# Two decode layers on one core: the order of MLP loads, of scores and transposes, and the filling of the weight ring

## The chip, the cores and the metric

The kernel runs on one core of one Trainium2 chip. The metric is the device time of one execution in microseconds, the median over runs. Five engines work side by side, each through its own queue in order: TensorE (PE, with its weight loads shown as PEld), VectorE (DVE), ScalarE (ACT), GpSimd (POOL) and SyncE (SP). SP does nothing here but issue DMAs; sixteen DMA engines carry each of them.

## What is computed

Two layers, each an attention over a cache and then a gated MLP, both with a layer norm in front and a residual sum behind. There are 4 sequences with one new token each, width 640, 32 heads of 128, a window of the last 1024 cached positions, and an MLP of 1728 hidden units. Everything is float32. Both layers use the same weights and the same cache.

```python
def _A_ref(x, k_cache, v_cache, wq, wo):
    q = (x @ wq).reshape(B, Sq, Hq, Dh).transpose(0, 2, 1, 3)
    k, v = k_cache[:, :, Sk - W:, :], v_cache[:, :, Sk - W:, :]     # W = 1024
    scores = jnp.einsum("bhqd,bhkd->bhqk", q, k) * (Dh ** -0.5)
    o = jnp.einsum("bhqk,bhkd->bhqd", softmax(scores), v)
    return o.transpose(0, 2, 1, 3).reshape(B, Sq, Hq * Dh) @ wo
def _B_ref(x, W_gate, W_up, W_down):
    gate, up = x @ W_gate, x @ W_up
    return (gate * (gate > 0) * up) @ W_down
x = x + _A_ref(_layernorm(x), ...)
x = x + _B_ref(_layernorm(x), ...)      # and both once more
```

## The kernel before, in words

The host lays the weights out so that each load is a plain block of 128 partitions. A head is 9472 columns of float32 per partition: 640 of Wq, 4096 of K, 4096 of V, 640 of Wo. The MLP's 1728 hidden units are cut into three blocks of 512 units (5120 columns of W_gate and W_up, then 2560 of W_down) and the 192 units that are left over. Of these the gate and up columns (1920) and the first 128 rows of W_down (640 columns) lie in the array `rest`, and the last 64 rows of W_down lie in the array `tail`, which is 64 partitions by 640.

In on-chip memory there is one tile, `store`, of 128 partitions by STORE columns (5.76 heads), used as a ring. The list `todo`, made by `pieces`, `half_a`, `half_b`, `ending` and `mlp`, says in which order the pieces are loaded; `load()` (line 129) takes the next piece, places it at `at`, and issues its DMA on SP (line 152) if those columns are free. `done()` frees columns once the matmul that reads them has been written, and calls `load()` again. A piece that would not fit before the end of the ring is cut at one of the places in `CUTS`; a piece whose columns are not all free waits whole. On the chip the DMA waits on SP for the PE instruction that read those columns last, and, since eight semaphores go round, for the eighth DMA before it. SP is in order, so what waits there holds up every later load.

Five heads (27 to 31) are kept on chip from layer 0 to layer 1 (of head 27 only Wq and K), in columns 0 to 42,624; layer 1 takes them first. So the MLP of layer 0 and the first heads of layer 1 have only the upper 12,000 columns to pass through, until layer 1 has used up the kept heads.

The order of work on the engines is the order of the program text (`manual_schedule`). `attention` (line 322) goes through the heads; one round for head h, with `after` = h + 1 and `before` = h − 1, is: `query` of after (`qp`, line 248), `turned` of h (eight transposes of the softmax weights `probs` into `pp`, line 284, copied to `pT`, line 285), `totals` and `values_turned` of before (`so`, lines 301 and 309), `query_turned` of after (`qt`), `project` of before (`y`, line 318), `scores` of after (`ps`, line 269, then the maximum `nm` on DVE, line 274, and the exponential into `probs` on ACT, line 276), and `values` of h (`po`, line 294, copied to `gates` on ACT, line 297). There is one `probs`, one `ps`, one `po` and one `gates`.

`forward` (line 354) is the MLP: `gate(j)` multiplies by W_gate and W_up of block j (`gu`, line 365; j = 3 is the left-over units), `gated` makes the hidden values, `hidden` transposes them (`ph`, `hT`), and `down` multiplies by W_down into the sum `y` (line 404). The norm in front of each is `normalized` (line 199) with `deviation`.

Of the kernel before, what the change touches and what calls it, by code (L numbers as in the profile page):

```python
# [7 lines left out]
F32 = mybir.dt.float32  # L8
# [19 lines left out]

STORE = 54600
# [5 lines left out]
FIRST, FIRST_MLP = 10960, 51152  # L37
# [5 lines left out]
    "rest": [*range(0, RGU, P), RGU, RGU + D],  # L43
    "tail": [0, D],
# [4 lines left out]
def decode_kernel(ctx: ExitStack, tc: tile.TileContext, x, heads, blocks, rest, tail, sel, out):  # L49
# [34 lines left out]
    def mlp(layer):  # L84
        fine = layer == 0
# [42 lines left out]
    source = {"head": heads, "block": blocks, "rest": rest, "tail": tail}  # L128
# [3 lines left out]
    def load():  # L132

        nonlocal at
        while todo:
# [6 lines left out]
            if any(live[at:at + hi - lo]):  # L142
                return
# [6 lines left out]
            p = 64 if kind == "tail" else P  # L150
            src = src[i][:, lo:hi] if kind in ("head", "block") else src[:, lo:hi]
            nc.sync.dma_start(out=store[:p, at:at + hi - lo], in_=src)
# [87 lines left out]
    qp, qs, qT, pT, sums, so, r, oT = {}, {}, {}, {}, {}, {}, {}, {}  # L240
# [21 lines left out]
    def scores(layer, h):  # L262
# [3 lines left out]
        for j in range(2):  # L266
            for b in range(B):
# [3 lines left out]
                done(key, lo, 512)  # L271
        nm = small.tile([P, 1], F32, name="nm")
        flat = ps.rearrange("p j n -> p (j n)")
# [48 lines left out]
    def attention(layer):  # L322
        hs = order[layer]
        xT, d = normalized()
# [5 lines left out]
        scores(layer, hs[0])  # L330
        for h, after, before in zip(hs, hs[1:], [None] + hs):
# [22 lines left out]
    def forward(layer):  # L354
        xT, d = normalized()
# [22 lines left out]
        def hidden(j, h):  # L378
            hTs[j] = small.tile([P, 4, B], F32, name="hT")
# [6 lines left out]
            for g in range(3):  # L386
                lo = 64 * (g % 2)
                nc.tensor.matmul(ph[lo:lo + 64, g // 2, :B], h, ident[:96, 32 * g:32 * g + B],
                                 start=True, stop=True, tile_position=(0, lo))
            nc.vector.tensor_copy(hTs[j][:, 0], ph[:, 0, :B])  # L390
            nc.vector.tensor_copy(hTs[j][:64, 1], ph[:64, 1, :B])

        def down(j, groups, last=False):
            for f in groups:
                p = P
                if j < 3:
                    key, lo = (layer, "block", j), GU + f * D
                elif f == 0:
                    key, lo = (layer, "rest", 0), RGU
                else:  # L400
                    key, lo, p = (layer, "tail", 0), 0, 64
                w = get(key, lo, D)
                for g in range(4):
                    nc.tensor.matmul(y[32 * g:32 * g + B], hTs[j][:p, f], w[:p, g * QUARTER:(g + 1) * QUARTER],  # L404
                                     start=False, stop=last and f == groups[-1], tile_position=(0, 32 * g))
                done(key, lo, D)

# [3 lines left out]
        h3 = gated(3)  # L411
        gate(0)
        hidden(3, h3)
        h0 = gated(0)
        down(3, [1, 0])
        gate(1)
        hidden(0, h0)
# [78 lines left out]
```

## Time and profile before

| what | before |
|---|---|
| median of 3 runs (757.96 to 759.31) | 757.97 us |
| the profiled execution's own time | 759.14 us |
| its span | 757.3 us |
| TensorE busy, mean granted clock | 576.2 us (76%), 0.838 |
| VectorE, ScalarE busy | 175.1 us (23%), 120.5 us (16%) |
| loads on the SP queue | 315.19 MB, 98.3% of 16 engines' span |

The page counts what the engines and the DMA engines did between the first and the last instruction. A row of a timeline has the start in us, the duration, the engine, the line, the operation and its tiles; in brackets stands how long the engine had been idle and what ended the wait. Matmuls of float32 appear as two instructions each. A row of the windows has the busy time of each engine, the granted TensorE clock, the mean busy share of the 16 DMA engines, and the GB/s that they moved.

### The profile page before, as it was taken

What the parts mean: (1) busy time and instruction counts of PE and PEld (TensorE: products, weight loads), DVE (VectorE), ACT (ScalarE), POOL (GpSimd) and SP (SyncE); (2) the same over time, 40 slices, a digit from 0 to 9 for tenths busy, and PEclk for the clock granted to TensorE, in tenths of its full rate; (3) what the DMA queues carried; (4) which work ended last, traced back from release to release, by engine and by line L of the source; (5) the groups of instructions that cost most, each with busy time, mean ns of one, the idle gap of its engine ahead of it and who ended that gap; (6) DMA issues with size and microseconds to landing.
All of it is one profiled execution on the core that took longest, in us unless ns stands there. A gap on an engine that the chain in (4) does not pass through costs nothing.

```text
span 757.3 us, 11694 instructions
## 1 busy us (share of the span) xinstructions
PE 576.2 (76%) x5146; PEld 317.1 (42%) x5146; DVE 175.1 (23%) x497; ACT 120.5 (16%) x214; POOL 0.2 (0%) x4
## 2 busy tenths in 40 slices
PE   0776777776797695798877888888778776795985
PEld 0343344344354253354433444444335344354442
DVE  0222222222222222223202223232222222221220
ACT  1111101011101101112201111211110111111120
POOL 0000000000000000000000000000000000000000
PEclk9888898788877979879976889999797788877898
DMA  9999999999999999999999999999999999999995
GB/s 389 438 416 440 428 433 429 429 432 428 435 427 428 432 435 426 425 428 421 362 395 422 365 415 426 428 440 426 425 433 433 431 429 432 429 428 424 420 398 211
DMA packets 18938, 316.02 MB, mean 417 GB/s; under 512 B 2116, under 2 KB 2756, under 8 KB 5832
## 3 DMA queue, kind: packets, MB, share of 16 engines
q1 hardware_dynamic: 18736, 315.19, 98.3%
q8 instruction: 40, 0.66, 0.4%
q10 hardware_dynamic: 152, 0.10, 0.0%
q14 instruction: 10, 0.08, 0.0%
HBM read 315.19 MB, written 0.08 MB: 416 GB/s over the span
## 4 chain that ended last, share of the span: by engine, by line
DMA 66%; PE 24%; DVE 5%; issue 3%; ACT 2%; ACTq 0%; DVEq 0%; SPq 0%
DMA store<-in_heads 58%; PE ps L269 7%; DMA store<-in_blocks 6%; PE pp L284 5%; PE so L309 4%; DVE nm L274 3%; DMA sel_sb<-in_sel 2%; PE y L318 2%; ACT probs L276 1%; PE qp L248 1%; PE qt L258 1%; DVE pT L285 1%; PE gu L365 1%; PE po L294 1%; PE y L404 1%
## 5 line engine op out<-in xcount | busy, mean ns | idle before, releaser
L269 PE MATMUL ps<-store,qT 128*32 128x512 f32 x1024 | 166.7, 783 | 1.0 <-DVE qT L260 1.0
L276 ACT ACTIVATE probs<-ps,nm 128x1024 f32<-128x1024 f32 x64 | 71.3, 1113 | 543.0 <-DVE nm L274 543.0
L294 PE MATMUL po<-store,pT 128*32 128x512 f32 x1024 | 123.6, 602 | 0.0
L274 DVE TENSOR_REDUCE nm<-ps 128x1 f32<-128x1024 f32 x64 | 78.4, 1225 | 184.9 <-PE ps L269 184.9
L248 PE MATMUL qp<-store,xT 128*32 128x128 f32 x640 | 45.1, 309 | 90.9 <-DMA store<-in_heads 89.6
L284 PE MATMUL pp<-sel_sb,probs 128*128 128x128 f32 x512 | 86.2, 323 | 23.3 <-ACT probs L276 23.2
L309 PE MATMUL so<-sel_sb,gates 128*128 128x1 f32 x512 | 80.4, 278 | 28.5 <-DVE r L303 25.2
L309 PEld LDWEIGHTS so<-sel_sb,gates 128*128 128x128 f32 x512 | 76.7, 230 | 32.9 <-issue 28.7
L248 PEld LDWEIGHTS qp<-store,xT 128*32 128x32 f32 x640 | 29.0, 118 | 139.3 <-issue 125.3
L284 PEld LDWEIGHTS pp<-sel_sb,probs 128*128 128x128 f32 x512 | 67.9, 164 | 40.9 <-ACT probs L276 33.5
L294 PEld LDWEIGHTS po<-store,pT 128*32 128x32 f32 x1024 | 34.2, 117 | 91.5 <-issue 90.8
L269 PEld LDWEIGHTS ps<-store,qT 128*32 128x32 f32 x1024 | 36.8, 135 | 71.6 <-issue 60.3
L254 DVE TENSOR_SCALAR qs<-qp,rstd 128x128 f32<-128x128 f32 x64 | 22.5, 351 | 152.4 <-PE qp L248 152.1
L285 DVE COPY pT<-pp 128x128 f32<-128x128 f32 x128 | 37.3, 292 | 65.5 <-PE pp L284 59.3
L297 ACT COPY gates<-po 128x512 f32<-128x512 f32 x64 | 36.9, 576 | 8.3 <-PE po L294 8.3
L318 PE MATMUL y<-store,oT 128*4 128x160 f32 x512 | 35.8, 360 | 1.6 <-DVE oT L312 0.5
L312 DVE TENSOR_TENSOR oT<-so,r 128x4 f32<-128x4 f32 x64 | 10.4, 162 | 98.1 <-PE so L309 98.1
L365 PE MATMUL gu<-store,xT 128*32 128x256 f32 (+1 forms) x300 | 22.6, 445 | 9.7 <-DMA store<-in_blocks 8.8
L258 PE MATMUL qt<-sel_sb,qs 128*128 128x4 f32 x128 | 28.3, 291 | 1.0 <-DVE qs L254 1.0
L258 PEld LDWEIGHTS qt<-sel_sb,qs 128*128 128x128 f32 x128 | 25.6, 248 | 1.6 <-ACT rstd L232 0.9
L301 PEld LDWEIGHTS so<-sel_sb,sm 128*128 128x128 f32 x128 | 24.0, 233 | 1.7 <-issue 1.7
L301 PE MATMUL so<-sel_sb,sm 128*128 128x4 f32 x128 | 21.1, 235 | 0.0
(49 smaller groups left out, 111.9 us busy)
## 6 DMA issues: line engine op xcount, KB each, us to landing
store<-in_heads SPq DMA_DIRECT2D x37, 4736.0 KB, 39.9
store<-in_heads SPq DMA_DIRECT2D x15, 2368.0 KB, 38.9
store<-in_heads SPq DMA_DIRECT2D x12, 1344.0 KB, 11.1
store<-in_heads SPq DMA_DIRECT2D x12, 1024.0 KB, 10.7
store<-in_blocks SPq DMA_DIRECT2D x3, 2560.0 KB, 26.9
store<-in_heads SPq DMA_DIRECT2D x2, 3648.0 KB, 38.9
store<-in_heads SPq DMA_DIRECT2D x2, 3392.0 KB, 37.8
store<-in_heads SPq DMA_DIRECT2D x1, 4656.0 KB, 39.6
```

The costliest lines, as they stand in the source:

```text
L248: nc.tensor.matmul(qp[h][32 * g:32 * g + 32, :], xT[:, c], w, start=c < 4, stop=c > 0, tile_position=(0, 32 * g))
L258: nc.tensor.matmul(qt, qs.pop(h), sel_b, start=True, stop=True)
L269: nc.tensor.matmul(ps[32 * b:32 * b + 32, j, :], q[:, b:b + 1].to_broadcast([P, 32]), get(key, lo, 512), start=True, stop=True, tile_posit ...
L274: nc.vector.tensor_reduce(nm, flat, axis=AX.X, op=ALU.max, negate=True)
L276: nc.scalar.activation(probs, flat, AF.Exp, bias=nm, accum_out=sums[h])
L284: nc.tensor.transpose(pp[:, c, :], probs[:, (4 * j + c) * P:(4 * j + c + 1) * P], ident)
L285: nc.vector.tensor_copy(t[:, 4 * j:4 * j + 4], pp[:, :, None, 0:P:32].to_broadcast([P, 4, 8, B]))
L294: nc.tensor.matmul(po[32 * g:32 * g + 32, :], p[:, c], get(key, VV + c * 512, 512), start=c < 4, stop=c >= 4, tile_position=(0, 32 * g))
L297: nc.scalar.copy(gates, po)
L301: nc.tensor.matmul(so[h][:, :B], sums.pop(h).to_broadcast([P, P]), sel_s, start=True, stop=True)
L309: nc.tensor.matmul(s[:, B + b:B + b + 1], gates[:, b * P:(b + 1) * P], sel_b[:, b:b + 1], start=True, stop=True)
L318: nc.tensor.matmul(y[32 * g:32 * g + B], o, get(key, WO + g * QUARTER, QUARTER), start=False, stop=last, tile_position=(0, 32 * g))
```

## The change

There are four edits. The `tail` array goes: its 64 rows of W_down are folded to 128 partitions by 320 columns and appended to `rest`, so that the left-over units are one load of 2880 columns (`REST`); `hidden(3)` writes its 64 left-over values to both halves of the partitions, and `down(3)` takes the upper and the lower half in four matmuls of 64 rows. In the MLP, in both layers, all of W_gate and W_up is loaded ahead of all of W_down, each in two pieces of 2048 and 3072 columns, and `down(0)` comes after `gate(2)` in the program. In a round of attention `scores` of head h + 1 comes ahead of `totals` and `turned` of head h, and the softmax is a function of its own behind these. And `load(True)` is called at the start of `attention` and `forward`: there a piece whose columns are only partly free is cut at the last place in `CUTS` that fits, if that is 512 columns or more. STORE is 40 columns smaller, FIRST and FIRST_MLP are other offsets.

```diff
+REST = RGU + D + 2 * QUARTER
-STORE = 54600
+STORE = 54560
-FIRST, FIRST_MLP = 10960, 51152
+FIRST, FIRST_MLP = 10928, 51688
...
-        gu = [0, GU * 2 // KC, GU] if fine else [0, GU]
-        pieces(layer, "rest", 0, 0, RGU)
+        gu = [0, GU * 2 // KC, GU]
+        pieces(layer, "rest", 0, 0, REST)
         pieces(layer, "block", 0, *gu)
-        pieces(layer, "tail", 0, 0, D)
-        pieces(layer, "rest", 0, RGU, RGU + D)
         pieces(layer, "block", 1, *gu)
+        pieces(layer, "block", 2, *gu)
         pieces(layer, "block", 0, GU, GU + WD)
-        pieces(layer, "block", 2, *gu)
         pieces(layer, "block", 1, GU, GU + WD)
         pieces(layer, "block", 2, GU, GU + 2 * D, GU + 3 * D, GU + WD)
...
-    def load():
+    def load(part=False):
...
             if any(live[at:at + hi - lo]):
-                return
+                n = live.index(True, at) - at
+                hi = max([lo] + [c for c in CUTS[kind] if c <= lo + n])
+                if not part or hi < lo + 512:
+                    return
...
             query(layer, after, xT)
             query_out(after, rstd)
-            turned(h)
             if before is not None:
-                totals(before)
                 values_turned(before)
             query_turned(after)
             if before is not None:
                 project(layer, before, False)
             scores(layer, after)
+            totals(h)
+            turned(h)
+            softmax(after)
             values(layer, h)
 
         before, h = hs[-2:]
-        totals(before)
+        totals(h)
+        turned(h)
         values_turned(before)
-        turned(h)
-        totals(h)
         values(layer, h)
...
+            if j == 3:
+                w = get(key, RGU + D, 2 * QUARTER)
+                for g in range(4):
+                    r = slice(64 * (g // 2), 64 * (g // 2) + 64)
+                    nc.tensor.matmul(y[32 * g:32 * g + B], hTs[j][r, 1], w[r, g % 2 * QUARTER:(g % 2 + 1) * QUARTER],
+                                     start=False, stop=False, tile_position=(r.start, 32 * g))
+                done(key, RGU + D, 2 * QUARTER)
...
+        h = gated(3)
+        for j, j1 in (3, 0), (0, 1), (1, 2):
+            gate(j1)
+            hidden(j, h)
+            h = gated(j1)
+            if j == 3:
+                down(3)
+        down(0)
+        hidden(2, h)
+        down(1)
+        down(2, last=True)
```

In the order that the built programs have, the rows of one engine stand one below the other; "x8" is eight equal instructions in a row. One round of attention on PE before (`qp`, `pp`, `so` for the totals, `so` for the values, `qt`, `y`, `ps`, `po` as above):

```order
L248 MATMUL qp<-store,xT 32x128 x5
L284 MATMUL pp<-sel_sb,probs 128x128 x8
L301 MATMUL so<-sel_sb,sm 128x4
L309 MATMUL so<-sel_sb,gates 128x1 x4
L258 MATMUL qt<-sel_sb,qs 128x4
L318 MATMUL y<-store,oT 4x160 x4
L269 MATMUL ps<-store,qT 32x512 x8
L294 MATMUL po<-store,pT 32x512 x8
```

The same round on PE in the changed kernel, whose line numbers are three higher from the softmax on:

```order
L248 MATMUL qp<-store,xT 32x128 x5
L312 MATMUL so<-sel_sb,gates 128x1 x4
L258 MATMUL qt<-sel_sb,qs 128x4
L321 MATMUL y<-store,oT 4x160 x4
L269 MATMUL ps<-store,qT 32x512 x8
L304 MATMUL so<-sel_sb,sm 128x4
L287 MATMUL pp<-sel_sb,probs 128x128 x8
L297 MATMUL po<-store,pT 32x512 x8
```

The totals and the transposes have moved from behind the query to behind the scores. On DVE the copies `pT` thereby stand directly ahead of the maximum `nm` (they stood behind `qs`, ahead of `oT`):

```order
L306 RECIPROCAL r<-so 128x4
L288 COPY pT<-pp 128x128 x2
L277 TENSOR_REDUCE nm<-ps 128x1
L254 TENSOR_SCALAR qs<-qp,rstd 128x128
L315 TENSOR_TENSOR oT<-so,r 128x4
L260 COPY qT<-qt 128x4
```

So the maximum over the new scores now waits for both copies of the head before.

The SP queue through the MLP of layer 0 before, from the load of the left-over units to the last of W_down (PE_49 is a wait for a PE instruction, DMAHW one for an earlier load):

```order
L152 DMA store_82<-in_rest 128x1920 [waits DMAHW6_49,PE_49]
L152 DMA store_82<-in_blocks 128x1280 [waits DMAHW7_49,PE_49]
L152 DMA store_82<-in_blocks 128x768 [waits DMAHW0_49]
L152 DMA store_82<-in_blocks 128x3072 [waits DMAHW1_49]
L152 DMA store_82<-in_tail 64x640 [waits DMAHW2_49]
L152 DMA store_82<-in_rest 128x640 [waits DMAHW3_49]
L152 DMA store_82<-in_blocks 128x2048 [waits DMAHW4_49]
L152 DMA store_82<-in_blocks 128x3072 [waits DMAHW6_49,DMAHW5_49,PE_49]
L152 DMA store_82<-in_blocks 128x1280 [waits DMAHW7_49,PE_49]
L152 DMA store_82<-in_blocks 128x1280 [waits DMAHW1_49,DMAHW0_49,PE_49]
L152 DMA store_82<-in_blocks 128x2048 [waits PE_49]
```

The same queue in the changed kernel:

```order
L152 DMA store_82<-in_rest 128x2560 [waits DMAHW7_49,PE_49]
L152 DMA store_82<-in_rest 128x320 [waits DMAHW0_49]
L152 DMA store_82<-in_blocks 128x2048 [waits DMAHW1_49]
L152 DMA store_82<-in_blocks 128x3072 [waits DMAHW2_49]
L152 DMA store_82<-in_blocks 128x2048 [waits DMAHW3_49]
L152 DMA store_82<-in_blocks 128x1536 [waits DMAHW4_49]
L152 DMA store_82<-in_blocks 128x1536 [waits DMAHW7_49,DMAHW5_49,PE_49]
L152 DMA store_82<-in_blocks 128x1280 [waits DMAHW6_49,PE_49]
L152 DMA store_82<-in_blocks 128x768 [waits DMAHW1_49,DMAHW0_49,PE_49]
L152 DMA store_82<-in_blocks 128x3072 [waits DMAHW2_49]
```

The `tail` load is gone, and the second 3072 columns of block 1 are cut in two at the norm, so that 1536 of them go out ahead of the first wait for the MLP's own matmuls. The load of 1280 columns behind that goes to ring columns 53,184 to 54,464, which hold the first W_down rows of the left-over units: the PE instruction that it waits for is `down(3)`, where the 1280 columns of before waited for `gate(0)`.

The end of the program on PE, in layer 1's MLP, before:

```order
L365 MATMUL gu<-store,xT 32x256 x20
L382 MATMUL ph<-sel_sb,gates 128x128
L404 MATMUL y<-store,hT 4x160 x16
L382 MATMUL ph<-sel_sb,gates 128x128
L404 MATMUL y<-store,hT 4x160 x16
```

and in the changed kernel:

```order
L371 MATMUL gu<-store,xT 32x256 x20
L388 MATMUL ph<-sel_sb,gates 128x128
L402 MATMUL y<-store,hT 4x160 x16
L388 MATMUL ph<-sel_sb,gates 128x128
L402 MATMUL y<-store,hT 4x160 x32
```

Between `gate(2)` and the end stood 32 matmuls of W_down (blocks 1 and 2); now there are 48 (all three blocks), and the loads of all three now come behind those of `gate(2)`.

More of the change, by code (lines that the diff above doesn't have):

```diff
@@ L42, with decode_kernel @@
     "block": [*range(0, GU, 256), *range(GU, GU + WD + 1, D)],
-    "rest": [*range(0, RGU, P), RGU, RGU + D],
-    "tail": [0, D],
+    "rest": [*range(0, RGU, P), RGU, RGU + D, REST],
 }
 @with_exitstack
-def decode_kernel(ctx: ExitStack, tc: tile.TileContext, x, heads, blocks, rest, tail, sel, out):
+def decode_kernel(ctx: ExitStack, tc: tile.TileContext, x, heads, blocks, rest, sel, out):
     nc = tc.nc
@@ L127, in decode_kernel @@
     at = FIRST
-    source = {"head": heads, "block": blocks, "rest": rest, "tail": tail}
+    source = {"head": heads, "block": blocks, "rest": rest}
     held = {}
-    def load():
+    def load(part=False):
         nonlocal at
@@ L149, in load @@
             src = source[kind]
-            p = 64 if kind == "tail" else P
-            src = src[i][:, lo:hi] if kind in ("head", "block") else src[:, lo:hi]
-            nc.sync.dma_start(out=store[:p, at:at + hi - lo], in_=src)
+            src = src[:, lo:hi] if kind == "rest" else src[i][:, lo:hi]
+            nc.sync.dma_start(out=store[:, at:at + hi - lo], in_=src)
             at += hi - lo
@@ L323, in attention @@
         hs = order[layer]
+        load(True)
         xT, d = normalized()
@@ L354, in forward @@
     def forward(layer):
+        load(True)
         xT, d = normalized()
```

51 lines of the change are left out of this document (15 added, 36 removed).

## Prediction

> **What bounds the kernel now.** I read the page first, then share and rate of the DMA engines by windows, then the chain of waits, and last the timeline of one round of attention.
>
> ```profile
> span 757.3 us, 11694 instructions
> q1 hardware_dynamic: 18736, 315.19, 98.3%
> DMA 66%; PE 24%; DVE 5%; issue 3%; ACT 2%; ACTq 0%; DVEq 0%; SPq 0%
> store<-in_heads SPq DMA_DIRECT2D x37, 4736.0 KB, 39.9
> 460.00:700.00 240.00, 190.57 (x1607) 104.89 (x1606) 59.15 (x160) 38.64 (x69) 0.00 (x0) 0.83 1.00 429
> 376.00:381.00 5.00, 4.48 (x78) 3.04 (x74) 1.30 (x7) 1.38 (x3) 0.00 (x0) 0.75 0.70 239
> 381.00:417.00 36.00, 24.45 (x308) 12.17 (x300) 5.73 (x22) 4.14 (x8) 0.00 (x0) 0.74 1.01 419
> 417.00:432.00 15.00, 13.23 (x122) 6.48 (x122) 4.72 (x12) 3.36 (x6) 0.00 (x0) 0.92 0.91 347
> 722.00:734.00 12.00, 9.18 (x126) 6.21 (x119) 2.71 (x13) 3.85 (x7) 0.00 (x0) 1.00 1.00 371
> 734.00:742.00 8.00, 7.42 (x137) 4.02 (x136) 1.45 (x7) 1.30 (x4) 0.00 (x0) 1.00 1.02 430
> ```
>
> The loads fill 98.3% of the DMA engines' span and two thirds of the chain: the kernel streams weights. The last two columns of a window are DMA share and GB/s. From 460 to 700 the share is 1.00 at 429 GB/s: nothing is to be had there. A head is issued 39.9 us before it lands, and its 4.85 MB take 11.3 us at 429 GB/s, so three heads wait in the queue and columns freed 3 us earlier or later are not noticed. Four places remain. The stream runs thin in the MLP of layer 0 (376 to 381, share 0.70) and early in layer 1 (417 to 432, 0.91); in the MLP of layer 1 it is busy but slow (722 to 734, 371 GB/s at share 1.00); and there is work behind the last load.
>
> ```profile
> 717.36 28.73 DMA store<-in_blocks
> 746.22 4.47 PE gu L365 x40
> 751.22 1.27 PE y L404 x32
> 729.21 0.33 SPq L152 DMA_DIRECT2D store<-in_blocks  x1
> store<-in_blocks SPq DMA_DIRECT2D x1, 320.0 KB, 23.1
> 753.02 1.31 PE y L404 x32
> 754.35 0.33 DVE probs L434
> ```
>
> The last load was issued at 729.21 and landed 23.1 us later, at 752.3. But PE takes up the last block of W_down only at 753.02: `gate(2)` could start at 746.22, when its weights had landed (717.36 + 28.73 = 746.09), and two blocks of W_down come after it.
>
> **The tail of layer 1.** Now 7680 columns of W_down (3.93 MB, 9.2 us at 429 GB/s) land behind the weights of `gate(2)`, whose 4.47 us are over well before them; each block of W_down costs PE 1.3 us, and its load 3.1. Behind the last landing there remain four matmuls, a quarter of 1.31 us, and some 0.1 us of wait: y ends 0.45 us after the landing instead of 2.0 (752.3 to 754.33). That is 1.5 us at full clock, and about 0.3 less if those matmuls run at half clock. I take 1.3. The copy and the store behind y stay.
>
> **The half load.** From 722 to 734, with the 64-partition `tail` load on its way, the stream loses 12 × (1 − 371/429) = 1.6 us; from 734 on, with 2560-column loads still coming, it runs at 430 again. The fold gives the same bytes to all partitions in longer rows, so it can lose nothing; the gain lies between 0 (another cause in that window) and 1.6. I take 1.4, near the upper end, because short rows alone did not slow the window after it. In layer 0 the same gain buys nothing by itself, for there the stream waits for PE.
>
> [...]
>
> **One round of attention.** Where PE is the slower side, the round decides when columns come free. At full clock, before:
>
> ```profile
> 424.42 1.02 PE so L309 x8
> 425.97 1.90 PE L269 MATMUL ps<-store,qT 128*32 128x512 f32 x16
> 428.00 1.22 DVE L274 TENSOR_REDUCE nm<-ps 128x1 f32<-128x1024 f32 x1 [2.14 <-PE ps L269]
> 429.32 1.11 ACT L276 ACTIVATE probs<-ps,nm 128x1024 f32<-128x1024 f32 x1 [6.14 <-DVE nm L274]
> 430.43 0.58 ACT L297 COPY gates<-po 128x512 f32<-128x512 f32 x1
> 430.58 1.09 PE L284 MATMUL pp<-sel_sb,probs 128*128 128x128 f32 x8 [0.58 <-ACT probs L276]
> 431.28 0.73 DVE L285 COPY pT<-pp 128x128 f32<-128x128 f32 x2 [0.88 <-PE pp L284]
> 431.51 0.28 PE L301 MATMUL so<-sel_sb,sm 128*128 128x4 f32 x2
> 432.24 1.05 PE L309 MATMUL so<-sel_sb,gates 128*128 128x1 f32 x8 [0.45 <-DVE r L303]
> ```
>
> From `ps` to `so` of the values 6.27 us, from there to the next `ps` 1.55 (424.42 to 425.97): 7.82, with PE idle for 0.58 + 0.45. After: `ps` about 1.7, totals 0.28, transposes until both copies are done 1.43 (430.58 to 432.01), together 3.4. Only then comes the maximum, 1.22; the exponential 0.10 later, 1.11; on ACT behind it the copy of `gates`, 0.58; `so` about 0.06 later, at 6.5; plus 1.55 makes 8.05. Both waits of PE are gone, and one of about 1.1 us for `gates`, with `so`, `qt` and `y` queued behind it, stands in their place: a round is 0.2 us longer, not shorter. What is won is a start, since `scores` no longer stand behind transposes that wait for a softmax.
>
> ```profile
> 322.49 1.91 PE pp L284 x8
> 324.98 1.84 PE so L309 x8
> 374.70 0.50 PE y L318 x8
> 383.50 0.84 PE L404 MATMUL y<-store,hT 64*4 64x160 f32 x16 [0.32 <-DVE hT L391]
> 389.14 12.66 DMA store<-in_blocks
> 414.55 1.98 PE pp L284 x8
> 416.99 3.17 PE ps L269 x16
> 427.07 0.33 SPq L152 DMA_DIRECT2D store<-in_heads  x1
> 427.00:428.00 1.00, 1.00 (x14) 0.26 (x8) 0.00 (x0) 0.00 (x0) 0.00 (x0) 1.00 0.24 81
> 428.00:429.00 1.00, 1.00 (x16) 0.28 (x12) 0.99 (x1) 0.00 (x0) 0.00 (x0) 1.00 1.03 226
> 719.00 1.90 PE L269 MATMUL ps<-store,qT 128*32 128x512 f32 x16
> 730.11 0.46 PE L318 MATMUL y<-store,oT 128*4 128x160 f32 x8 [0.26 <-DVE oT L312]
> ```
>
> **From layer 0 to layer 1** these shifts add up on one chain, and where it ends is where the stream starts anew.
> The end of attention, 375.2 before: `scores` of head 27 2.5 us earlier (322.49 to 324.98); the round behind it, partly at half clock, 1.3 longer (with 2.9 for `ps` and 2.3 for transposes and copies, as at 416.99 and 414.55, the sum above gives 10.3 instead of 9.0); three more rounds, 0.2 each; the end, 719.00 to 730.57 or 11.6 in layer 1, about 1.0 longer, since the last softmax now waits for the transposes of the head before. Together +0.4.
> The MLP of layer 0: 1536 columns more go out before PE begins (0.79 MB, 1.8 us), but the 1280 columns two places on now wait for `down(3)`, the first half of the row at 383.50, so until 383.9 + 0.4 = 384.3. All later loads of SP are queued behind; between, the stream has one load of 1536 columns. A restart costs 1.0 us from issue, and 0.5 more at the reduced rate (427.07, then 81 and 226 GB/s): in effect 385.8. From there 12,800 columns (6.55 MB) at 419 GB/s end at 401.4, with landing and the engines' spread about 402.4; before, the last landing was 389.14 + 12.66 = 401.8. So layer 1 starts 0.6 later (0 to 2).
> Early in layer 1: `scores` of head 28 no longer wait for the transposes, 2.4 earlier (414.55 to 416.99), the round behind it 1.3 longer. The load that waits at 427.07 for head 29's K is then issued at 427.07 + 0.6 − 1.1 = 426.6. By that time the stream is at 385.8 + 34,432 columns (17.6 MB) at 419 GB/s = 427.9, so it does not run dry a second time: full rate from about 428.0 where it was 428.5 before. The gain is 0.5 us. Its bounds: the whole loss of the two windows, 5 × (1 − 239/429) + 15 × (1 − 347/429) = 5.1 us won; and 2.5 us lost, if start and wait go wrong by 2 and the rounds by 0.2 each.
>
> **What is hidden or nothing.** The filling at the norms cuts a load in attention and MLP of layer 0 and none in layer 1, by the order; in the first it only splits a load that stands far ahead in the queue. The number of loads is the same. The extra matmul of `hidden(3)` and the copy that is saved (0.1 us each) lie in the wait above. In all other rounds the 39.9 us of queue cover the 0.2.
>
> **The sum.** 0.5 + 1.4 + 1.3 = 3.2 us. The profiled execution took 759.14, 1.8 more than its span and 1.2 more than the median: 759.1 becomes 755.9, and the median 757.97 becomes 754.8. Less than 0.2% (1.5 us) can't be told from no change here.
>
> **Rivals.**
> *The vector engine's order makes the rounds slow (slower).* The maximum behind two copies and `gates` behind the exponential leave PE idle 1.1 us at a stretch; if its clock is then at half more often, `ps`, transposes and `so` double on that path. By the restart some six rounds have passed; it becomes slower than now by 0.2% where each takes 0.8 us more than I reckon. At 1.0 more the transition costs 5.5, the time is 760.8. Against it: PE was idle for as much in a round before, at clock 0.92.
> *The wait for `down(3)` counts in full.* If head 29 comes no earlier, both stalls stand: about 2 us lost in place of 0.5 won, 757.3.
> [...]
> *Both thin windows fill.* If PE runs the left-over units at full clock, `down(3)` comes 1.5 us earlier and half of the 5.1 us is won: 752.8.
>
> **How the numbers follow.** Forecast 0.43, slow rounds 0.18, the wait in full 0.15, own bytes only 0.14, both filled 0.10. Nearly all of the first and last, and three quarters of the fourth, are faster: 0.64; the wait in full is mostly the same: 0.17; slow rounds give 0.19 with the rest. The likeliest alone spans 753.3 to 756.4. The range reaches down to the filled windows and up over the wait in full into the slow rounds: 752.3 to 759.5.
>
> **What the profile will show.** `y` ends about 0.5 us after the last landing; the MLP of layer 1 runs at over 420 GB/s throughout; rounds near 8 us with PE waiting for `gates` ahead of `so`; one gap in the loads between 381 and 386, none near 420. I am wrong if the gap is longer than 5 us, if rounds reach 9 us at full clock, or if the rate in layer 1's MLP stays at 400.

## The result, and the profile after

The changed kernel takes 759.13 us (median of 12 runs, 754.85 to 761.78); the kernel before, beside it, 757.97 (12 runs). The ratio, which is not the quotient of the two medians, is 1.0005 with a 95% interval of 0.9981 to 1.0029: no difference that can be told, and at most 1.4 us won where 3.2 were forecast. Six of the 12 runs took 754.9 to 757.8 us and six 760.4 to 761.8, so the median lies between two groups and no run took it. The profile is of one that took 760.87, and so shows what the slower half loses.

The page of the changed kernel, and its windows (busy time of PE, PEld, DVE, ACT and POOL, granted clock, DMA share, GB/s):

```profile
span 758.8 us, 11659 instructions
q1 hardware_dynamic: 18864, 315.19, 98.0%
DMA 54%; PE 31%; DVE 5%; ACT 5%; issue 4%; SPq 0%; ACTq 0%; DVEq 0%
376.00:381.00 5.00, 4.44 (x62) 3.52 (x61) 1.28 (x7) 1.42 (x3) 0.00 (x0) 0.50 0.70 256
381.00:384.00 3.00, 3.00 (x42) 1.34 (x34) 0.06 (x1) 0.00 (x0) 0.00 (x0) 0.69 0.62 240
384.00:386.00 2.00, 1.73 (x40) 0.92 (x40) 0.45 (x2) 0.37 (x1) 0.00 (x0) 1.00 0.03 8
386.00:388.00 2.00, 2.00 (x37) 0.93 (x27) 0.00 (x0) 0.12 (x1) 0.00 (x0) 1.00 0.89 223
417.00:432.00 15.00, 12.94 (x100) 6.35 (x104) 3.04 (x9) 2.63 (x5) 0.00 (x0) 0.77 0.93 364
460.00:700.00 240.00, 198.13 (x1632) 99.04 (x1624) 60.04 (x162) 40.36 (x72) 0.00 (x0) 0.84 1.00 429
722.00:734.00 12.00, 11.01 (x94) 5.22 (x95) 3.15 (x10) 1.68 (x3) 0.00 (x0) 0.88 1.01 420
734.00:742.00 8.00, 6.56 (x87) 4.69 (x83) 1.77 (x9) 2.73 (x5) 0.00 (x0) 0.71 1.01 424
```

The loads' part of the chain has fallen from 66% to 54%, and TensorE's has grown from 24% to 31%. From 722 to 734 the stream now runs at 420 GB/s, where it ran at 371. But in the MLP of layer 0 there are two microseconds with next to no transfer (384 to 386, 8 GB/s), and two more at about half the rate.

The chain of waits, at both ends of a layer (start, duration, what the time went to):

```profile
377.46 1.92 PE gu L371 x25
380.68 3.37 PE gu L371 x40
385.17 4.30 DMA store<-in_blocks
390.64 14.42 DMA store<-in_blocks
...
738.52 1.92 PE gu L371 x25
741.74 3.75 PE gu L371 x40
746.93 2.30 PE gu L371 x40
749.48 2.29 PE gu L371 x40
752.04 1.20 PE y L402 x32
753.50 2.33 PE y L402 x64
```

In layer 0, `gate(3)` takes 1.92 us at halved clock (0.50) and `gate(0)` 3.37 with a clock of 0.68 over it; `down(3)` comes behind them, and the load that waits for it is issued at 385.17. The last load of this MLP lands at 390.64 + 14.42 = 405.06 (401.8 before). In layer 1 the chain no longer ends with a load: from 738.52 to the end of `y` at 755.83 it is TensorE's own work, though the last load landed at 754.5.

Two rounds of attention in layer 1 (timeline of TensorE):

```profile
427.26 1.05 PE L312 MATMUL so<-sel_sb,gates 128*128 128x1 f32 x8 [1.04 <-ACT gates L300]
435.29 1.05 PE L312 MATMUL so<-sel_sb,gates 128*128 128x1 f32 x8 [1.02 <-ACT gates L300]
436.87 3.06 PE L269 MATMUL ps<-store,qT 128*32 128x512 f32 x16
444.96 1.05 PE L312 MATMUL so<-sel_sb,gates 128*128 128x1 f32 x8 [1.02 <-ACT gates L300]
```

The first takes 8.03 us, at full clock (1.00), with one wait of 1.0 us for `gates`; the second, in which the clock is at half (0.50) from 437.46 to 440.88 and `ps` takes 3.06 us instead of 1.90, takes 9.67.

### The profile page after: what moved, and what is told of

It is laid out like the page before. It is cut to its first block, busy times and chain, and to the rows that moved or that the text cites. A ratio compares the mean times of both kernels' runs of the same rounds, so it can differ in the third digit from the quotient of the medians.

```text
span 758.8 us, 11659 instructions
## 1 busy us (share of the span) xinstructions
PE 604.1 (80%) x5150; PEld 303.2 (40%) x5150; DVE 174.9 (23%) x495; ACT 120.6 (16%) x214; POOL 0.2 (0%) x4
## 4 chain that ended last, share of the span: by engine, by line
DMA 54%; PE 31%; DVE 5%; ACT 5%; issue 4%; SPq 0%; ACTq 0%; DVEq 0%
DMA store<-in_heads 52%; PE ps L269 10%; PE so L312 6%; DVE nm L277 5%; PE pp L287 5%; DMA store<-in_blocks 2%; PE y L321 2%; ACT probs L279 2%; PE gu L371 2%; ACT gates L300 2%; PE so L304 2%; PE qt L258 1%; PE qp L248 1%; PE po L297 1%; PE y L402 1%
## 5 line engine op out<-in xcount | busy, mean ns | idle before, releaser
L269 PE MATMUL ps<-store,qT 128*32 128x512 f32 x1024 | 185.5, 861 | 4.4 <-ACT probs L279 3.9
L297 PE MATMUL po<-store,pT 128*32 128x512 f32 x1024 | 126.2, 611 | 0.0
L312 PE MATMUL so<-sel_sb,gates 128*128 128x1 f32 x512 | 80.3, 278 | 29.5 <-ACT gates L300 29.4
L312 PEld LDWEIGHTS so<-sel_sb,gates 128*128 128x128 f32 x512 | 75.0, 225 | 47.0 <-ACT gates L300 40.2
L287 PE MATMUL pp<-sel_sb,probs 128*128 128x128 f32 x512 | 77.3, 300 | 0.0
L287 PEld LDWEIGHTS pp<-sel_sb,probs 128*128 128x128 f32 x512 | 71.4, 173 | 0.0
L306 DVE RECIPROCAL r<-so 128x4 f32<-128x4 f32 x64 | 11.7, 183 | 221.6 <-PE so L304 221.6
L297 PEld LDWEIGHTS po<-store,pT 128*32 128x32 f32 x1024 | 27.1, 110 | 50.8 <-DVE pT L288 29.5
L304 PE MATMUL so<-sel_sb,sm 128*128 128x4 f32 x128 | 29.9, 304 | 1.9 <-ACT probs L279 1.9
```

Of the source, the lines that this page charges most:

```text
L269: nc.tensor.matmul(ps[32 * b:32 * b + 32, j, :], q[:, b:b + 1].to_broadcast([P, 32]), get(key, lo, 512), start=True, stop=True, tile_posit ...
L287: nc.tensor.transpose(pp[:, c, :], probs[:, (4 * j + c) * P:(4 * j + c + 1) * P], ident)
L297: nc.tensor.matmul(po[32 * g:32 * g + 32, :], p[:, c], get(key, VV + c * 512, 512), start=c < 4, stop=c >= 4, tile_position=(0, 32 * g))
L304: nc.tensor.matmul(so[h][:, :B], sums.pop(h).to_broadcast([P, P]), sel_s, start=True, stop=True)
L312: nc.tensor.matmul(s[:, B + b:B + b + 1], gates[:, b * P:(b + 1) * P], sel_b[:, b:b + 1], start=True, stop=True)
```

## Experiments

Each kernel was run beside the kernel before, and its ratio is to that. In the table stand the median, the ratio with its interval, the median of the granted clock over the runs, and then, from the one profiled execution, how far the stream of loads is ahead (+) or behind (−) the kernel before at five times. That is worked out from the packets of the load queue: the MB moved up to that time, less those of the kernel before, at 0.429 MB per us. The profiled execution need not be a typical one: that of *old rounds* took 756.04 us (median 758.71), that of *folded load cut* 758.82 (757.04).

| kernel | us | ratio | clock | 376 | 386 | 402 | 722 | 734 |
|---|---|---|---|---|---|---|---|---|
| changed | 759.13 | 1.0005 (0.9981–1.0029) | 0.831 | +0.8 | −1.8 | −3.3 | −3.9 | −2.6 |
| old rounds | 758.71 | 1.0006 (0.9987–1.0024) | 0.847 | +0.5 | +0.8 | +0.9 | −0.5 | +0.9 |
| only new rounds | 757.53 | 0.9987 (0.9972–1.0001) | 0.832 | +0.1 | −0.1 | −0.0 | +0.3 | +0.5 |
| `gates` on DVE | 756.67 | 0.9974 (0.9957–0.9992) | 0.842 | +0.5 | +0.2 | −0.3 | −0.9 | +0.5 |
| `down(3)` early | 760.01 | 1.0016 (0.9994–1.0038) | 0.825 | +0.7 | −1.3 | −1.9 | −2.9 | −1.6 |
| fold only | 755.28 | 0.9958 (0.9940–0.9975) | 0.848 | +0.6 | +0.4 | +0.4 | +0.5 | +1.9 |
| W_down last only | 759.35 | 1.0003 (0.9986–1.0019) | 0.850 | −0.2 | −0.1 | −0.1 | −1.2 | −1.4 |
| DVE, old MLP 0 | 756.90 | 0.9981 (0.9963–0.9999) | 0.843 | +0.6 | −1.8 | −3.4 | −1.3 | −0.0 |
| fill | 754.24 | 0.9968 (0.9938–0.9998) | 0.928 | +2.0 | −1.5 | −1.5 | +1.1 | +2.6 |
| folded load cut | 757.04 | 0.9979 (0.9962–0.9996) | 0.832 | +0.6 | −1.6 | −2.1 | −2.2 | −0.9 |
| fold, new rounds, fill | 755.35 | 0.9956 (0.9939–0.9972) | 0.859 | +0.4 | −2.6 | −2.5 | −0.8 | +0.6 |
| fold, old rounds, fill | 756.25 | 0.9972 (0.9950–0.9994) | 0.887 | +0.5 | −1.7 | −1.7 | −0.7 | +0.7 |
| fill, folded load cut | 754.47 | 0.9937 (0.9911–0.9962) | 0.924 | +2.0 | +2.5 | +2.5 | +3.1 | +4.6 |

One column can be read at once: between 722 and 734 every kernel with the fold gains 1.3 to 1.5 us on the kernel before, and the two without it gain 0.2 and lose 0.2.

### Four first guesses: the rounds or the wait

The first trace offered two suspects, the new round with its wait for `gates`, and the wait for `down(3)`. *Old rounds* is the changed kernel with the order of attention of before; *only new rounds* the kernel before with the new order of attention. (In the texts on record the kernel named as changed is that of 759.13 us.)

```diff
 # old rounds
             query_out(after, rstd)
+            turned(h)
             if before is not None:
+                totals(before)
                 values_turned(before)
...
             scores(layer, after)
-            totals(h)
-            turned(h)
-            softmax(after)
             values(layer, h)
```

> The changed kernel with the rounds of attention in the order of before; loads, fold, filling and the MLP's order stay as changed. Theory R (the new round is what costs: transposes, copies, maximum, exponential and the copy of the values now stand on one chain, PE idles about 1.1 us at a stretch and its clock is at half more often, so the end of attention in layer 1 is 6 us late): the MLP of layer 1 begins near 733 instead of 738.5, y ends 0.5 us after the last landing, and the time is 3 us under the kernel before, about 755. Theory S (the stall of the loads in the MLP of layer 0, while SP waits for down(3), is what costs): the stall stays, and the time stays within 1 us of the changed kernel. Theory L (no part costs; the runs fall into two groups by the phase of the clock): the same two groups 5 us apart as the changed kernel has.

Measured: 758.71, as slow as the changed kernel. Its profile is of an execution of 756.04, the second fastest of 12, and shows what a good run looks like (chain of waits):

```profile
376.03 1.09 PE gu L367 x25
377.81 2.34 PE gu L367 x40
381.26 5.23 DMA store<-in_blocks
387.66 13.01 DMA store<-in_blocks
```

Here `gate(3)` and `gate(0)` ran at full clock (1.00 from 376 to 384), the load behind `down(3)` went out at 381.26, before the stream was dry, and the last load landed at 400.67. Putting the old round back takes nothing from the median, against theory R, so the new order by itself is not what cost the gain. Its runs lie between 755.8 and 762.2 without the two groups of theory L; what the slower ones lose, no profile shows.

> The kernel before with nothing but the new order of a round. R: the rounds where PE is behind the loads take 9.2 us on average instead of 8.6, scores of head 29 in layer 1 come 1 to 2 us later, the end of attention in layer 1 about 6 us later; since the end of layer 1 waits for gate(2)'s weights anyway, the time is 1 to 4 us above before. S: no stall is added, the start of scores is won, so 0 to 1 us below before. L: no difference in the mean, but two groups of runs.

Measured: 757.53, 0.9987 (0.9972 to 1.0001). The new round alone does no harm, although it lowers the median clock from 0.85 to 0.83.

*`gates` on DVE* and *`down(3)` early* are the changed kernel with one edit each:

```diff
 # gates on DVE
-        nc.scalar.copy(gates, po)
+        nc.vector.tensor_copy(gates, po)
 # down(3) early
+            if j == 3:
+                hidden(j, h)
+                down(3)
             gate(j1)
-            hidden(j, h)
+            if j < 3:
+                hidden(j, h)
             h = gated(j1)
-            if j == 3:
-                down(3)
```

> The changed kernel with the copy of the values (gates) on the vector engine, behind the maximum, instead of behind the exponential on ACT. R: so no longer waits for the exponential, a round at full clock falls from 8.0 to about 7.3 us, at mixed clock from 9.2 to 8.5; the end of attention in layer 1 comes 3 us or more earlier, the time falls by 2 to 4 us against the changed kernel, to 755 to 757. S: the stall stays, the time within 1 us of the changed kernel.

> The changed kernel with hidden(3) and down(3) ahead of gate(0) in the MLP's program, so that the load that waits for down(3) is issued some 2.4 us earlier (gate(0) took 3.4 us, the wait for the hidden values costs PE about 1). S: the stall between 381 and 386 shrinks by 2.4 us, layer 1 starts as much earlier, and the time falls by 2 us or more. R: the last landing may come 1 to 2 us earlier, but PE at the end of layer 1 is what ends the kernel, so at most 1 us in the mean.

Measured: 756.67 (0.9974, 0.9957 to 0.9992) and 760.01 (1.0016, 0.9994 to 1.0038). The first is faster than the kernel before, as theory R said; its interval overlaps that of the changed kernel a little. The group of `so` of the changed kernel, and of this one (busy us, mean ns, idle time ahead of it):

```profile
L312 PE MATMUL so<-sel_sb,gates 128*128 128x1 f32 x512 | 80.3, 278 | 29.5 <-ACT gates L300 29.4
```

```profile
L312 PE MATMUL so<-sel_sb,gates 128*128 128x1 f32 x512 | 82.4, 282 | 10.5 <-DVE gates L300 10.5
```

The idle time falls from 29.5 us to 10.5; how much of the gain that makes is not shown. Moving `down(3)` forward did not help, against theory S. It did shorten the wait: the load behind it is issued 4.9 us after the start of `gate(3)` (383.77 − 378.91), where the changed kernel took 7.7 (385.17 − 377.44). But its profile is of an execution of 761.40, in which TensorE came to this MLP 1.5 us later; the stream still loses 2.0 us between 376 and 386, and `hidden(3)` now waits 0.56 us for the vector engine.

### The parts one by one

*Fold only* and *W_down last only* are each the kernel before with one part of the change.

```diff
 # fold only
-        pieces(layer, "tail", 0, 0, D)
-        pieces(layer, "rest", 0, RGU, RGU + D)
+        pieces(layer, "rest", 0, RGU, REST)
 # W_down last only
-        pieces(layer, "block", 0, GU, GU + WD)
         pieces(layer, "block", 2, *gu)
+        pieces(layer, "block", 0, GU, GU + WD)
...
-        down(0, range(4))
         gate(2)
         hidden(1, h1)
         h2 = gated(2)
+        down(0, range(4))
```

> The kernel before with one edit: the 64 left-over rows of W_down are folded to 128 partitions and loaded with the rest of that block; everything else as before. If the half-filled load slows its neighbours, as the 371 GB/s between 722 and 734 say, the MLP of layer 1 runs above 415 GB/s there, the last landing comes 1.4 us earlier and the time is 1.4 below the kernel before (756.6 beside 758.0, ratio 0.998). [...] If those 12 us are slow for another cause, the rate stays near 371 and nothing is won.

Measured: 755.28, ratio 0.9958 (0.9940 to 0.9975), 3.2 us faster, more than twice what I expected. The window, and `gate(2)` and the end of `y` in the timeline, fold only:

```profile
722.00:734.00 12.00, 9.17 (x123) 6.42 (x126) 2.63 (x13) 3.97 (x8) 0.00 (x0) 0.96 1.00 424
743.20 2.37 PE L364 MATMUL gu<-store,xT 128*32 128x256 f32 x40 [0.16 <-DMA store<-in_blocks]
749.88 0.46 PE L395 MATMUL y<-store,hT 128*4 128x160 f32 x8 [0.27 <-DMA store<-in_blocks]
```

And `gate(2)` of the kernel before:

```profile
746.22 4.47 PE L365 MATMUL gu<-store,xT 128*32 128x256 f32 x40 [4.15 <-DMA store<-in_blocks]
```

The rate goes from 371 to 424 GB/s. The packets of the load queue show that the loads beside the half load were slowed: those of 20,480 bytes took 0.93 us on average between 722 and 729 in the kernel before, and 0.77 with the fold. Short rows are not the cause, for packets of 2,560 bytes took 0.10 us between 742 and 748 in the kernel before, and 0.14 between 722 and 729. Then comes what I had not reckoned with. Before, TensorE was idle for 4.15 us ahead of `gate(2)`, and ran it at about half clock (0.52 over its 4.47 us). With the fold its weights come 3.0 us earlier, TensorE is idle for 0.16 us and takes 2.37. So `y` ends 0.5 us behind the last landing (749.88) without any other order of loads: the landing is 2.4 us earlier (752.3 before), and the work behind it 1.5 shorter.

> The kernel before with one edit: W_down after all of W_gate and W_up in both layers; the half-filled load and the old round stay. By the forecast's term for the tail, y ends about 0.5 us after the last landing instead of 2.0, which is 1.3 us (756.7 beside 758.0). If the later release of columns in the MLP of layer 0 takes more than that from the start of layer 1, the time is 758.0 or above and the load that ran dry near 427 is issued later than in the kernel before.

Measured: 759.35, 1.0003 (0.9986 to 1.0019). W_down last only, the same window and the end:

```profile
722.00:734.00 12.00, 9.60 (x98) 4.93 (x90) 2.92 (x9) 3.27 (x6) 0.00 (x0) 0.98 1.01 366
744.45 2.37 PE L364 MATMUL gu<-store,xT 128*32 128x256 f32 x40
753.89 0.46 PE L403 MATMUL y<-store,hT 128*4 128x160 f32 x8 [0.34 <-DMA store<-in_blocks]
```

Without the fold the 366 GB/s stay. The tail does what I said, `y` ends 0.5 us after the last landing; but this landing is at 753.85, 1.5 us later than before, and the gain is gone. (`gate(2)` takes 2.37 us here too: with W_down behind it, its weights come early enough.) The stream falls behind by some tenths at a time (0.4 at 432, 0.9 at 460, 1.4 at 734). The load that ran dry near 427 is issued at 427.33, 0.3 us later than before, and the two behind it at 429.04 and 430.80, 1.1 and 1.2 us later; in this execution TensorE's clock was 0.50 from 425.6 to 429.0. Whether the other executions lose their time there, no run shows.

### The whole load and its wait

*DVE, old MLP 0* has `gates` on DVE and keeps, in layer 0 alone, the MLP's order of before. *Folded load cut* is the changed kernel with the folded load in two pieces:

```diff
 # DVE, old MLP 0
+        if layer:
+            pieces(layer, "block", 2, *gu)
         pieces(layer, "block", 0, GU, GU + WD)
+        if not layer:
+            pieces(layer, "block", 2, *gu)
 # folded load cut
-        pieces(layer, "rest", 0, 0, REST)
+        pieces(layer, "rest", 0, 0, RGU)
         pieces(layer, "block", 0, *gu)
+        pieces(layer, "rest", 0, RGU, REST)
```

> The changed kernel with two edits: gates is copied by the vector engine, and in layer 0 alone the MLP keeps the order of before (W_down of block 0 ahead of W_gate and W_up of block 2); layer 1 has W_down last. Beside the kernel that has only the first edit (756.67): if the order in layer 0 costs about 1 us at the restart, 755.5; if it costs nothing, 756.7; if the old order frees the columns for layer 1 later, above 757.

Measured: 756.90, like `gates` on DVE alone. The order of W_down in layer 0 is not the cause: the load behind `down(3)` waits as before (issued at 385.93), because the W_down part of the left-over units still lies at the front of the ring. This kernel shows one thing more. At 402 its stream is as late as the changed kernel's (−3.4 and −3.3), yet the load that ran dry near 427 goes out at 427.20 (427.07 in the kernel before, 429.94 in the changed kernel), and at 722 it is 1.3 us behind instead of 3.9. So the lag at 402 does not settle the time by itself; it matters also how fast TensorE is in the first rounds of layer 1 (its clock from 417 to 432 was 0.89 here, 0.77 in the changed kernel).

> The changed kernel with one edit: the folded load is cut in two, so that the W_down part of the left-over units is loaded after block 0's W_gate and W_up, as before. The load that waited for down(3) (issued at 385.17 in the changed kernel, 2.6 us without a transfer behind it) then waits only for the first matmuls of gate(0). If that wait is where the gain went, the stream is at most 1 us behind the kernel before at 402 (3.3 behind in the changed kernel), and the median is 2 to 3 us below the changed kernel's: 756 to 757. Rival, the gain goes where TensorE with its clock halved is late, whatever the load waits for: the lag at 402 stays above 2 us and the median near 759.

Measured: 757.04, 0.9979 (0.9962 to 0.9996), 2.1 us below the changed kernel, as the text said; the two intervals overlap. The lag at 402 did not come out: it is 2.1 us, where at most 1 was expected and the rival said above 2. Chain of the kernel with the folded load cut:

```profile
379.94 1.92 PE gu L372 x25
383.17 3.33 PE gu L372 x40
391.50 12.33 DMA store<-in_blocks
```

In this execution TensorE was at half clock in `gate(3)` and most of `gate(0)` (0.50 from 380 to 384, 0.85 from 384 to 388) as in the changed kernel's, and began 2.5 us later. Yet the last load of the MLP landed at 403.83, 23.9 us after the start of `gate(3)`, where the changed kernel took 405.06 − 377.46 = 27.6. The kernel before took 24.6 (401.8 − 377.16), *old rounds*, with the wait but at full clock, 400.67 − 376.03 = 24.6. So the wait for `down(3)` cost nothing where `gate(0)` ran at full clock, and 3.7 us in this pair, where it ran at half for the most part. One pair is little, though. Over all the profiles this stretch took 24.6 to 27.6 us with the wait (*fill* 25.5, *DVE, old MLP 0* 26.0, `gates` on DVE 26.7) and 23.5 to 26.0 without it (*W_down last only* 26.0).

### The clock

Over the 12 runs of the changed kernel the time and the granted clock go together (correlation −0.87); over the 34, 35 and 27 runs of the kernel before in three comparisons they do not (−0.16, −0.22, 0.23). *Fill* is the changed kernel with six matmuls with a zero weight added to each round, where TensorE waits for `gates`:

```diff
+    def fill(n):
+        for _ in range(n):
+            nc.tensor.matmul(y, zero.to_broadcast([P, P]), sel_sb[:, :QUARTER], start=False, stop=False)
...
             if before is not None:
+                fill(6)
                 values_turned(before)
```

> The changed kernel with six more matmuls with a zero weight into y in each round of attention, ahead of the matmuls that wait for gates; the result does not change. Theory of the clock: the wait of 1.1 us for gates lets TensorE's activity fall until its clock is halved, and the half-clock stretches make it late at both ends of a layer. With the wait filled the mean granted clock rises from 0.83 to above 0.85, and the time falls to 755 to 757. Rival, TensorE is simply late by the amount of work on it: six matmuls of about 0.14 us add 0.8 us to each round in which it is late, the clock stays near 0.83 and the time is 760 or more.

Measured: 754.24, 0.9968 (0.9938 to 0.9998). The group of `ps` in four kernels (line, count, busy us, mean ns, idle time ahead of it): before, changed, `gates` on DVE, and fill; then fill's matmuls behind `gates`, and its steady window.

```profile
L269 PE MATMUL ps<-store,qT 128*32 128x512 f32 x1024 | 166.7, 783 | 1.0 <-DVE qT L260 1.0
```

```profile
L269 PE MATMUL ps<-store,qT 128*32 128x512 f32 x1024 | 185.5, 861 | 4.4 <-ACT probs L279 3.9 <-DVE qT L260 0.5
```

```profile
L269 PE MATMUL ps<-store,qT 128*32 128x512 f32 x1024 | 174.7, 814 | 4.8 <-ACT probs L279 3.7 <-DMA store<-in_heads 0.6 <-DVE qT L260 0.5
```

```profile
L271 PE MATMUL ps<-store,qT 128*32 128x512 f32 x1024 | 134.1, 645 | 4.2 <-ACT probs L281 3.7 <-DVE qT L262 0.5
L314 PE MATMUL so<-sel_sb,gates 128*128 128x1 f32 x512 | 65.4, 249 | 1.0 <-ACT gates L302 1.0
460.00:700.00 240.00, 212.41 (x1886) 132.60 (x1882) 59.20 (x161) 38.67 (x69) 0.00 (x0) 0.94 1.01 431
```

More work, a faster clock: 133.8 us of added matmuls, and the granted clock goes from 0.83 to 0.93, `ps` from 185.5 to 134.1 us. The idle time ahead of `so` falls from 29.5 us to 1.0: between these two kernels the low clock goes with TensorE's idle time. The time falls by 0.37% against the changed kernel, with intervals that overlap a little, and the rival, that the added work itself makes TensorE late, falls for the median. But it does not fall altogether: the 12 runs lie between 751.5 and 762.0, five of them above 758, at clocks of 0.917 to 0.928. What happens in those five, no profile shows.

Two kernels add the fill to the fold alone, with three matmuls a round:

```diff
 # fold, new rounds, fill: the fold, the new order of a round, and
+                fill(3)
                 values_turned(before)
 # fold, old rounds, fill: the fold, the old order of a round, and
+            fill(2)
             turned(h)
...
+                fill(1)
                 values_turned(before)
```

> The kernel before with the fold, the new round of attention, and three zero-weight matmuls (0.95 us) in each round ahead of those that wait for gates; W_down keeps its place and no load is cut at the norms. If the fold's gain and that of a steady clock add up: granted clock above 0.88, 752 to 754, below the fold alone (755.3). If three matmuls don't hold the clock up, it stays below 0.85 and the time is that of the fold alone, 755 to 756.

> The kernel before with the fold and the old round, and three zero-weight matmuls in each round: two ahead of the transposes that wait for probs (0.58 us), one ahead of the matmuls that wait for r (0.45 us). If idle time of TensorE is what halves the clock in either order: clock above 0.88 and 752 to 754. If the old round is bound by its chain through the softmax, the clock rises and the time stays at 755 to 756, that of the fold alone.

Measured: 755.35 at a clock of 0.859, and 756.25 at 0.887. Neither is below the fold alone. Three matmuls raise the clock of the new round only in part (0.832 in *only new rounds*, 0.928 with six), and with the old round a clock of 0.89 buys nothing. The text's reason, that this round is bound by its chain through the softmax, is not shown.

The last kernel joins six matmuls and the folded load cut in two:

> The changed kernel with two edits tried apart so far: six zero-weight matmuls in each round ahead of those that wait for gates (754.24 alone), and the folded load cut in two, so that no load waits for down(3) (757.04 alone, 2 below the changed kernel). If the two losses are separate, the clock of TensorE and the wait for down(3), the clock is near 0.93, the stream is ahead of the kernel before at 402, and the median is 752 to 753. If the clock alone was the cause, so that the wait costs nothing once TensorE is fast, 754 as with the six matmuls alone. If the six matmuls of 0.32 us make TensorE late where it is the slower side, which the runs of 758 to 762 of that kernel would then show, the spread stays and the median is 754 or more.

Measured: 754.47 (6 runs, 751.45 to 756.6), 0.9937 (0.9911 to 0.9962). Window and chain of it, and the window of fill alone:

```profile
376.00:386.00 10.00, 9.73 (x152) 4.97 (x144) 1.44 (x6) 1.30 (x4) 0.00 (x0) 0.83 0.95 346
733.62 1.92 PE gu L380 x25
736.84 3.18 PE gu L380 x40
746.57 1.20 PE y L411 x32
748.02 2.33 PE y L411 x64
```

```profile
376.00:386.00 10.00, 9.13 (x151) 5.98 (x154) 1.69 (x9) 1.69 (x4) 0.00 (x0) 0.83 0.52 165
```

The gap in layer 0 is gone (346 against 165 GB/s), and the stream is 4.6 us ahead at 734. In the stream, then, the two losses are separate. But the time is that of the fill alone, not the 752 to 753 expected of separate losses; in this profile TensorE is the limit at the end: the last load lands at 746.2 and `y` ends at 750.35, after `gate(3)` of 1.92 us and `gate(0)` of 3.18 (1.09 and 2.34 at full clock in *old rounds*), with a clock of 0.71 from 734 to 742. This kernel, the fold alone, and the fold with new rounds and fill have intervals that lie wholly below the changed kernel's; from each other they can't be told.

## Why the prediction was right and wrong

- **The time.** 759.13 lies in the range of 752.3 to 759.5, at its upper end; the forecast of 754.8 and the 0.64 for faster were too hopeful. That the range holds the time is owed to the rivals that drew its upper end, not to the sum. Two of them lie about equally near: *the wait for `down(3)` counts in full* (757.3), whose price was too low, as the third point shows, and *slow rounds* (760.8 where each takes 1.0 us more).
- **The half load: right.** 1.4 us by the forecast; 12 × (420 − 371)/429 = 1.4 in the changed kernel, and 1.4 by the table for the fold only. The case *own bytes only*, which had a chance of 0.14, did not come, and no run shows what these bytes cost by themselves: at 429 GB/s the load's 160 KB need 0.38 us, and the fold won 1.4. That the loads beside it are slowed stands in the packets above (0.93 us against 0.77 for 20,480 bytes); why, no run here shows. The forecast's argument against short rows was weaker than it looked: in the kernel before, the shortest rows that move between 734 and 742 are of 7,680 bytes; those of 2,560 bytes come from 742 on.
- **From layer 0 to layer 1: wrong, +0.5 forecast, −3.3 at 402 in the profile.** Right in it: the end of attention (375.23, forecast 375.6), and that the load waits for `down(3)` (385.17; 384.3 forecast). Wrong was the step from there, "in effect 385.8": the loads behind it move 8 GB/s until 386 and 223 until 388, and the last landing is 405.06, not 402.4. I gave this step 0 to 2 us; here it cost about 3 (27.6 us from `gate(3)` to the last landing, 24.6 before), and nothing in *old rounds*, by the clock in `gate(0)`, which I had taken from one execution. The second dry spell, which I had argued away, came too: the load near 427 went out at 429.94 instead of 426.6. From the last landing to this load the changed kernel takes 24.9 us (429.94 − 405.06), 25.3 before, 24.2 by the forecast. That the first loss must reach this load is not so: *DVE, old MLP 0* lands late as well (404.23) and takes 23.0.
- **The tail: mechanism right, cause wrong.** W_down last does let `y` end 0.5 us after the landing, as that kernel alone shows. But the order was not the only cause of the late end before: `gate(2)` took 4.47 us, with the clock at 0.52 behind 4.15 idle microseconds, a row whose doubled duration I had quoted and not asked about. With the fold alone it takes 2.37, and `y` ends 0.5 us after the landing in the old order. So the term of 1.3 us was not the order's alone to win. In the changed kernel the term is lost again, since TensorE comes to layer 1's MLP 6.0 us later than before (738.52 against 732.55) and ends it 1.3 us behind the landing. `gate(3)` of the kernel before, in the timeline:

```profile
732.55 1.18 PE L365 MATMUL gu<-store,xT 128*32 128x128 f32 x27 [0.44 <-DVE d L225]
```

- **The round: right at full clock, 8.03 us against 8.05.** The rival *the vector engine's order makes the rounds slow* named the right danger, clocks at half more often, and the clock is indeed lower (0.83 against 0.85 with the new round alone). By itself it did not decide: the new round alone takes nothing, the old round gives nothing back. Together with the other parts it counts for something: a shorter wait for `gates` (0.9974) and the filled wait (0.9968) are both faster than the kernel before, where the changed kernel is not.
- **Open.** The fold alone gives 0.42%, the fold with all but the new round nothing (*old rounds*, 1.0006; the intervals lie apart). Between these two stand W_down last, the one load, the filling at the norms, and small matters (layer 1's W_gate and W_up in two pieces, the ring's offsets), and the loss is there. Cutting the folded load gives back 0.26% by the ratios, within the uncertainty of both. The filling at the norms was not tried alone, and why W_down last makes the stream late is not settled.

The three terms were worked out one by one, but those for the start of layer 1 and for the tail hung on the same clock, and the half load's 1.4 us can't show in the time where the stream has lost 3.9 before it.

## What to carry to other kernels

Where a matmul group takes twice its usual time, ask first how long TensorE was idle ahead of it: here `gate(2)` took 2.37 us instead of 4.47 once its weights came earlier, by the fold or by the order of the loads, and matmuls of no effect in the waits brought the mean of `ps` from 861 to 645 ns. When pieces are merged into one load, look at what frees the columns that this load lies in: here a part used only by `down(3)` held the next load back until 385.17, and from 384 to 386 the stream moved 8 GB/s. Try the parts of a change singly; here one part was worth 3.2 us and the whole nothing.

## What the runs showed of the hardware

- TensorE's clock fell to half (0.50) for a few microseconds at a time. Windows of the changed kernel:

```profile
464.00:466.00 2.00, 1.98 (x20) 0.66 (x24) 0.16 (x1) 0.00 (x0) 0.00 (x0) 0.69 0.97 409
466.00:468.00 2.00, 2.00 (x11) 0.60 (x4) 0.00 (x0) 0.00 (x0) 0.00 (x0) 0.50 1.00 419
468.00:470.00 2.00, 2.00 (x20) 1.22 (x24) 1.36 (x4) 0.00 (x0) 0.00 (x0) 0.95 1.00 413
```

  With half clock where it falls below 1, that is (0.31 + 0.50 + 0.05) × 2 × 2 = 3.4 us at half, though TensorE is busy for 5.98 of these 6 us; its last wait ahead of them, 1.02 us for `gates`, ended at 462.72. From 460 to 533 no wait of TensorE was longer than 1.04 us in the changed kernel, nor than 0.58 in the kernel before, and the mean clock there was 0.86 and 0.91. With the waits for `gates` filled (*fill*) the clock was 0.94 from 460 to 700, where the changed kernel had 0.84, and 0.93 against 0.83 over the runs.
- One load of 160 KB to 64 partitions cost the stream 1.4 us between 722 and 734 (*fold only* goes from 0.5 us ahead to 1.9, with 424 GB/s in place of 371), nearly four times the 0.38 us that its own bytes need at 429 GB/s.
